# RWKV-7 chunks and dropless experts on one core: a planned order with shared PSUM banks, page balance, later weights, and the first sums on GpSimd

## Chip, core and metric
One NeuronCore of a Trainium2 chip. The metric is the device time of one launch in microseconds; the kernel before takes 901.5 us (median of three runs, 900.42 to 902.14).

## The reference
Two blocks in a row, all float32. The first is a linear-attention recurrence over 768 steps for 4 batches x 8 heads, with a 40 x 40 state per head; the second sends each of the 3072 rows (320 wide) to the best of 8 experts.

```python
for t in range(S):
    y[:, :, t] = einsum('bhd,bhde->bhe', r_t, state)
    Sa = einsum('bhde,bhe->bhd', state, a_t)
    state = state * w_t[:, :, None, :] - einsum('bhd,bhe->bhde', Sa, b_t) + einsum('bhd,bhe->bhde', v_t, k_t)
x = y.transpose(0, 2, 1, 3).reshape(B * S, H * D)
e = argmax(x @ w_gate); p = softmax(x @ w_gate)[e]
out = p * (relu(x @ w1[e]) @ w2[e])
```

## The kernel before
**Units.** The attention part works in 24 units: 12 chunks of 64 steps, for two halves of the batch (`unit(u)`, u = 2·chunk + half). A unit loads seven blocks of 160 KB (decay, K, A, B, V twice, R), four DMAs each. From the decay VectorE makes running products: the scan `rv` (line 432), its reciprocal (437) and the scan `q` (440). GpSimd multiplies K and B (447, two halves) and A (449) by them. TensorE then makes K·A, masked to Gk (464), and B·A in both orientations, masked to T and N (481). The inverse of I + N is built by doubling: the squares of T and N, the first sums I + T (line 505, function `sums`, instructions at 488 and 491), then rounds that each make a power, copy it out, and add to the sum; the last round gives M and TT, and their product is TF. From it come u (641), z (masked to ZU, 663), y and the new state (689). A late step turns y to rows, makes the gate's logits, and SyncE stores 128 rows to memory.

Each fp32 matmul of a 64 x 64 tile stands in the trace as two weight loads and two matmuls, so a step of 16 such products is 32 + 32 instructions. `TILES` makes four neighbouring products use the four quarters of the array; K·A alternates over two of them. All matmul steps are recorded at line 385 (transposes at 573 and 583), all copies out of PSUM at 380 (ScalarE) and 382 (VectorE), all zeros at 350 to 358.

**Order.** Every operation is a `Step` (line 192) with a rank, an engine (ANY is ScalarE or VectorE), a planned cost, and what it reads and writes. `in_order` (212) plays the steps through a small model and emits each engine's instructions in the order in which the model starts them: of all ready steps, the one that can start earliest, then the one of lowest rank. Ranks are the unit's number, u - 3 for loads, u - 1 for the scans and products, u + 1 for the late steps. Hence a step without a predecessor goes as soon as its engine would be idle. The model also hands out PSUM: a step that opens a block of 1 or 2 of the 8 banks waits until such a block is free. For TensorE it counts pages of instructions (`PAGE, FETCH = 256, 3.6`, line 183; `n` is the number of instructions of a step): the next page may be entered 3.6 us after the last one was. On the chip the queues run in this order, each engine waiting on semaphores.

Tiles come from rings (line 320 on): A, R, KB, Vu of three buffers, V2, decay, rv of two, q of three. A load of unit u waits for the readers of the buffer's last use. SyncE issues nearly all loads; ScalarE those of B, A and R of unit 0 (line 424).

**Beginning.** GpSimd first fills constants, among them those that only the routing after the attention part uses (`before`, `ones_sq`, `zero_e`, `keep`, the counted ones at 127 and 128, `tokc`, `tokv`; lines 87 to 147) and `turn_gate` (150 to 157, with two loads from ScalarE's queue). Then come the zeros of the rings as steps of rank -100 to -50, on GpSimd and VectorE. The first expert's weights (2.3 MB) are a SyncE step of rank 8 without a predecessor (`first_weights`, 751).

**After.** Routing (763 to 867) sorts the rows, and the expert part (870 to 987) gathers, multiplies and scatters them.

Of the kernel before, what the change touches and what calls it, by code (L numbers as in the profile page):

```python
# [23 lines left out]
def kernel(  # L24
# [23 lines left out]
    nc = tc.nc  # L48
# [38 lines left out]
    before = consts.tile([128, 128], F32)  # L87
    nc.gpsimd.memset(before[:], 1.0)
    nc.gpsimd.affine_select(
        before[:], before[:], compare_op=ALU.is_gt, fill=0.0, base=0, pattern=[[1, 128]], channel_multiplier=-1,  # L90
    )

# [22 lines left out]

    ones_sq = consts.tile([128, 128], F32)
    nc.gpsimd.memset(ones_sq[:], 1.0)
    zero_e = consts.tile([128, E], F32)
    nc.gpsimd.memset(zero_e[:], 0.0)
    keep = consts.tile([128, E, NT], F32)  # L120
    nc.gpsimd.memset(keep[:], 1.0)
    nc.gpsimd.memset(keep[:, :, 0:1], 0.0)

    def counted(name, shape, pattern, base, mult=0):
        ti = consts.tile(shape, I32, name=name + "_i")
        tf = consts.tile(shape, F32, name=name)
        nc.gpsimd.iota(ti[:], pattern=pattern, base=base, channel_multiplier=mult)
        nc.gpsimd.tensor_copy(tf[:], ti[:])
        return tf
# [9 lines left out]
    iota_r = consts.tile([128, 128], F16)  # L139
    nc.gpsimd.tensor_copy(iota_r[:], iota_f[:])  # L140
# [3 lines left out]
    nc.gpsimd.tensor_scalar(tokc[HP:], tokc[HP:], scalar1=float(S - C), scalar2=None, op0=ALU.add)  # L144
    tokv = consts.tile([128, NT], F32)
    nc.gpsimd.tensor_copy(tokv[:, :NCH], tokc[:])
    nc.gpsimd.tensor_scalar(tokv[:, NCH:], tokc[:], scalar1=-1.0, scalar2=None, op0=ALU.mult)
# [3 lines left out]
    nc.gpsimd.memset(turn_gate[:, :, 128:], 0.0)  # L151
    for par in range(2):
        nc.scalar.dma_start(
            turn_gate[par * HP : par * HP + D, :, 128:], moe_w_gate.rearrange("(p a e) n -> a e p n", a=2, e=D)[par],
        )
    nc.gpsimd.tensor_scalar(turn_gate[:, :, 128:], turn_gate[:, :, 128:], scalar1=-1.0, scalar2=None, op0=ALU.mult)
    nc.gpsimd.tensor_copy(turn_gate[:, :, :128], ident[:, None, :].to_broadcast([128, NP, 128]))
# [25 lines left out]
    PAGE, FETCH = 256, 3.6  # L183
# [28 lines left out]
    def in_order():  # L212
# [3 lines left out]
        page = [0, 0.0]  # L216
# [26 lines left out]
        while ready:  # L243
            times = sorted({f for f in bank_free if f is not None})
            best = None
            for s, r in ready.items():
                new = [h for h in s.ps if h.at is None]
                for e in ((ACT, DVE) if s.eng == ANY else (s.eng,)):
# [13 lines left out]
                    key = (t0, s.rank, t0 + cost)  # L262
# [38 lines left out]
    with tc.tile_pool(name="ring", bufs=1) as ring, \  # L301
# [23 lines left out]
        r_dec = Ring("dec", [SEG * C1 + 1], 2)  # L325
# [34 lines left out]
        for i in range(3):  # L360
            for j, r in enumerate((r_KB, r_A, r_V2, r_Vu, r_R)):
                if i < len(r.bufs):
                    t, held = r.bufs[i]
                    for lo in (32, 96):
                        zero(-99 + 9 * i + j, POOL if lo == 32 else DVE, 0.5, t[lo : lo + 32], held)
        for t, held in r_qini.bufs:
            zero(-98, POOL, 0.6, t[:], held)
        for r in (r_rhs, r_ST, r_S):
            for t, held in r.bufs:
                zero(-50, POOL, 0.6, t[:], held)  # L370
# [4 lines left out]
        def pair(h, width):  # L375
            return psum[:, h.at : h.at + 2, : NP * width].rearrange("x a (p d) -> x a p d", p=NP)
# [18 lines left out]
        def unit(u):  # L395
# [28 lines left out]
            other = ACT if u == 0 else SP  # L424
# [14 lines left out]
            Step(pre, DVE, 0.3, invert, reads=hrv, writes=hqi + hpc)  # L439
# [17 lines left out]

            def p_ka(e, ps=ps):
# [4 lines left out]
            Step(u, PE, 8 * ROUND, p_ka, reads=hKB + hA, writes=[ps], n=64)  # L463
            Step(u, DVE, 0.69, lambda e, ps=ps: nc.vector.tensor_tensor(
                Gk[:], psum[:, ps.at, :].rearrange("x (q p j) -> x q p j", p=NP, q=2),
                m_plus[:, None, None, :].to_broadcast([128, 2, NP, C]), op=ALU.mult,
            ), reads=[ps], writes=hGk)
            T1, hT1 = r_T.take()
            N1, hN1 = r_N.take()
            for t1, ht1, mask, turned_ in ((T1, hT1, m_up, False), (N1, hN1, m_low, True)):  # L470
                ps = Held(2)

                def p_n(e, ps=ps, turned_=turned_):
                    t = pair(ps, C)
                    for p in range(NP):
                        for par, z in TILES:
                            q = par ^ z
                            l, r = b_at(p, q, par), head(Aq, p, q, par)
                            mm(t[halves[z], q, p, :], *((r, l) if turned_ else (l, r)))
                Step(u, PE, 4 * ROUND, p_n, reads=hKB + hA, writes=[ps], n=64)  # L480
                Step(u, DVE, 0.69, lambda e, ps=ps, t1=t1, mask=mask: nc.vector.tensor_tensor(  # L481
                    t1[:], pair(ps, C), mask[:, None, None, :].to_broadcast([128, 2, NP, C]), op=ALU.mult,
                ), reads=[ps], writes=ht1)
# [3 lines left out]
            def sums(e, dst, src, old, o):  # L487
                nc.vector.tensor_tensor(dst[:, 0], src[:, 0], old[:, 0], op=ALU.add)  # L488
                for h in range(2):
                    o_ = halves[1 - h]  # L490
                    nc.vector.tensor_tensor(dst[o_, 1], src[o_ if o else halves[h], 1], old[halves[h], 1], op=ALU.add)  # L491
# [530 lines left out]
```

## Time and profile before
| | us |
|---|---|
| median of three runs | 901.5 |
| profiled execution, its own time | 899.75 |
| its span, first to last instruction | 898.0 |
| attention part, to the last row turned (TensorE) | 574.63 + 2.18 |
| TensorE busy in the span (matmul records) | 776.2 |
| VectorE, ScalarE, GpSimd busy | 460.0, 234.5, 173.7 |
| mean granted clock of TensorE | 0.955 |

The 1.75 us between the profiled execution's time and its span lie around the instructions. Busy time is a share of stages that have different limits: TensorE's 86% is some 90% in the attention part, where many small matmuls overlap, little in the routing (572 to 620 us), and nearly full in the expert part. A granted clock of 1.00 is TensorE's upper level of 2.4 GHz, 0.5 the lower of 1.2 GHz, and a stretch's value is the mean. In rows on stretches the columns are the stretch, its length, then busy time and instructions of TensorE's matmuls, its weight loads, VectorE, ScalarE and GpSimd, the mean clock, the share of the DMA engines and GB/s. "Issue" ahead of an instruction is time in which its engine waited for nothing that the profile shows.

### The profile page before, as it was taken

The page shows a single profiled execution, that of the slowest core. Times are in us where ns is not written, and L with a number is a line of the kernel's source. Part 1 is how long each engine was busy: PE and PEld are TensorE (multiplying, and loading weights), DVE is VectorE, ACT ScalarE, POOL GpSimd, SP SyncE. Part 2 cuts the span into 40 slices and gives each one's busy share as a digit, 9 for nine tenths or more (in the row PEclk, how much of TensorE's full clock was granted, in tenths as well). Part 3 has the DMA queues.
Part 4 walks back from the last instruction along what each step waited for, and adds up shares of the span by engine and source line. Part 5 has one row for each costly group of instructions (what it writes and reads, how often), then busy time and mean ns, then how long its engine had stood idle before and what let it go on. Part 6 is the DMA issues. An engine that isn't in the chain of part 4 may idle for free.

```text
span 898.0 us, 38059 instructions
## 1 busy us (share of the span) xinstructions
PE 776.2 (86%) x17128; PEld 606.5 (68%) x17128; DVE 460.0 (51%) x980; ACT 234.5 (26%) x502; POOL 173.7 (19%) x224
## 2 busy tenths in 40 slices
PE   0797789889998999899989998418999999999995
PEld 0686678788887888788878887416845545545543
DVE  6685578777676867687767676361110110120110
ACT  0343244333333334333433433100110110110110
POOL 9332111121202020202020100043211211001001
PEclk9999899999999989999999999656999999999998
DMA  5323313222322232223222200183313513402000
GB/s 165 89 67 86 86 45 69 65 65 60 71 67 61 57 71 64 56 61 75 62 57 60 48 12 12 22 259 96 95 53 107 187 60 114 132 14 83 10 13 23
DMA packets 136569, 65.16 MB, mean 73 GB/s; under 512 B 116881, under 2 KB 132243, under 8 KB 136404
## 3 DMA queue, kind: packets, MB, share of 16 engines
q1 hardware_dynamic: 130888, 52.76, 23.2%
q0 software_dynamic: 3136, 9.44, 3.4%
q8 instruction: 135, 2.21, 1.0%
q10 hardware_dynamic: 2380, 0.50, 0.3%
q14 instruction: 30, 0.25, 0.1%
HBM read 54.01 MB, written 9.31 MB: 71 GB/s over the span
## 4 chain that ended last, share of the span: by engine, by line
issue 36%; PE 30%; DVE 11%; DMA 9%; POOL 7%; SPq 3%; ACT 2%; POOLq 0%; ACTq 0%; DVEq 0%
PE ps L385 25%; DMA dec<-in_packed_dram 8%; PE ps L583 4%; DVE X L491 3%; POOL out_dram L917 3%; SPq L416 3%; POOL xg L875 2%; PE ps L573 2%; ACT X L380 2%; DVE X L488 1%; DVE q L440 1%; DVE T L481 1%; POOL KB L447 1%; DMA KB<-in_packed_dram 1%; DVE TT L491 0%
## 5 line engine op out<-in xcount | busy, mean ns | idle before, releaser
L385 PE MATMUL ps<-X 64*64 64x64 f32 (+1 forms) x6144 | 163.1, 243 | 22.2 <-DVE X L491 10.9
L385 PEld LDWEIGHTS ps<-X 64*64 64x64 f32 x6144 | 133.8, 135 | 42.2 <-DVE X L491 15.4
L901 DVE TENSOR_SCALAR h_sb<-hp 128x448 f32<-128x448 f32 (+2 forms) x44 | 21.8, 497 | 227.1 <-PE hp L900 225.8
L910 PE MATMUL zp<-w,h_sb 128*128 128x320 f32 (+1 forms) x512 | 123.8, 433 | 0.0
L380 ACT COPY X<-ps 128x512 f32<-128x512 f32 x152 | 88.3, 586 | 125.6 <-PE ps L385 119.9
L894 PE MATMUL hp<-xgT,w 128*128 128x448 f32 (+2 forms) x352 | 115.0, 473 | 3.7 <-DVE h_sb L901 2.3
L910 PEld LDWEIGHTS zp<-w,h_sb 128*128 128x128 f32 (+1 forms) x512 | 80.6, 177 | 37.5 <-issue 2.4
L894 PEld LDWEIGHTS hp<-xgT,w 128*128 128x128 f32 x352 | 60.9, 208 | 53.1 <-issue 48.9
L447 POOL TENSOR_TENSOR KB<-KB,rv 128x512 f32<-128x512 f32 x48 | 59.0, 1249 | 133.9 <-DMA A<-in_packed_dram 48.6
L449 POOL TENSOR_TENSOR A<-A,q 128x512 f32<-128x512 f32 x24 | 29.2, 1215 | 248.9 <-PE ps L385 83.8
L917 POOL DMA_INDIRECT out_dram<-zo,s_idx x28 | 27.6, 987 | 185.1 <-ACT zo L916 183.8
L491 DVE TENSOR_TENSOR X<-ps,X 64x256 f32<-64x256 f32 x144 | 60.8, 422 | 3.1
L902 ACT ACTIVATE h_sb<-hp 128x448 f32<-128x448 f32 (+2 forms) x44 | 19.3, 442 | 159.9 <-PE hp L900 121.6
L488 DVE TENSOR_TENSOR X<-ps,X 128x256 f32<-128x256 f32 x72 | 30.4, 422 | 46.4 <-ACT X L380 45.8
L385 PE MATMUL ps<-R,Vu 64*128 64x64 f32 x768 | 51.0, 284 | 2.5 <-issue 1.2
L385 PE MATMUL ps<-A,KB 64*64 64x64 f32 x1536 | 45.3, 224 | 9.0 <-DVE M L524 8.4
L385 PEld LDWEIGHTS ps<-R,Vu 64*128 64x128 f32 x768 | 47.4, 196 | 5.0 <-issue 2.4
L385 PEld LDWEIGHTS ps<-A,KB 64*64 64x64 f32 x1536 | 40.6, 138 | 12.0 <-DVE M L524 8.6
L432 DVE TENSOR_TENSOR_SCAN rv<-dec,ones 128x521 f32<-128x521 f32 x24 | 29.7, 1239 | 34.7 <-DMA dec<-in_packed_dram 22.8
L663 DVE TENSOR_TENSOR ZU<-ps,m_plus 128x512 f32<-128x512 f32 x48 | 30.9, 685 | 28.8 <-PE ps L385 28.6
L916 ACT COPY zo<-zp 128x320 f32<-128x320 f32 x28 | 11.9, 425 | 119.8 <-PE zp L910 115.9
L385 PE MATMUL ps<-ZU,nKB 128*64 128x104 f32 (+1 forms) x768 | 39.6, 257 | 1.0 <-DVE ZU L663 0.8
(178 smaller groups left out, 1066.1 us busy)
## 6 DMA issues: line engine op xcount, KB each, us to landing
w<-in_moe_w_dram SPq DMA_DIRECT2D x8, 1280.0 KB
w<-in_moe_w_dram SPq DMA_DIRECT2D x8, 1024.0 KB
KB<-in_packed_dram SPq DMA_DIRECT2D x188, 40.0 KB
x_rows<-xs SPq DMA_DIRECT2D x48, 96.0 KB
dec<-in_packed_dram SPq DMA_DIRECT2D x96, 40.0 KB
V<-in_packed_dram SPq DMA_DIRECT2D x96, 40.0 KB
Vu<-in_packed_dram SPq DMA_DIRECT2D x96, 40.0 KB
A<-in_packed_dram SPq DMA_DIRECT2D x92, 40.0 KB
```

The source lines that it names most:

```text
L380: nc.scalar.copy(dst, src)
L385: nc.tensor.matmul(out_, lhsT=lhsT, rhs=rhs, start=start, stop=stop, skip_group_check=True)
L432: Step(pre, DVE, 1.4, lambda e: nc.vector.tensor_tensor_scan(rv[:, : SEG * C1 + 1][:, ::-1], dec[:, ::-1], ones65[:, ::-1], 0.0, op0=ALU.m ...
L447: Step(pre, POOL, 1.25, lambda e, kb=kb, by=by: nc.gpsimd.tensor_tensor(kb, kb, by, op=ALU.mult), reads=hrv, writes=hKB[i : i + 1])
L449: Step(pre, POOL, 1.22, lambda e: nc.gpsimd.tensor_tensor(Aq[:], Aq[:], q3[:, :, :C], op=ALU.mult), reads=hq, writes=hA)
L488: nc.vector.tensor_tensor(dst[:, 0], src[:, 0], old[:, 0], op=ALU.add)
L491: nc.vector.tensor_tensor(dst[o_, 1], src[o_ if o else halves[h], 1], old[halves[h], 1], op=ALU.add)
L583: nc.tensor.transpose(psum[:, ps.at + b // NP, b % NP * 128 : (b % NP + 1) * 128], at(*divmod(b, 2)).rearrange("x s t -> x (s t)"), ident[:],)
L663: Step(u, DVE, 0.69, lambda e, s=s, ps=ps: nc.vector.tensor_tensor(ZU[:, s, :, :C], psum[:, ps.at + s, :].rearrange("x (b j) -> x b j", j= ...
L894: nc.tensor.matmul(hp[:, : c1 - c0], lhsT=w[0][:, db, (fb + i) * 128 : (fb + i + 1) * 128], rhs=xT[:, db, c0:c1], start=(db == 0), stop=False,
L910: nc.tensor.matmul(zp[r0 : r0 + n], lhsT=h[:, fb, c0 : c0 + n], rhs=w[2][:, fb, :], start=(fb == 0), stop=(fb == FB - 1), skip_group_check ...
L917: ins_ = nc.gpsimd.indirect_dma_start(out=out[:, :], out_offset=bass.IndirectOffsetOnAxis(ap=si, axis=0), in_=zo[:], in_offset=None, bound ...
```

## The change
- `in_order`: among steps that can start at the same time, the rank has a term `uneven` added: how far TensorE's cost would run off from `PACE` (0.0134 us) per instruction. The first page counts as holding 190 instructions.
- Costs of steps are set anew: sums 1.29 (from 1.1), transposes 0.59 and 1.02, z 1.93, the row turn 1.12, K·A 1.0, large zeros 0.9.
- The two orientations of B·A become one step of 128 instructions into one block of two banks (T in the first half of each bank, N in the second; the products alternate); the two squares likewise, one after the other; and in the last round the sum, then the power. Masks and copies wait for the whole step.
- The state's share of y (`p_yr`) is no longer a step ahead of z, but the first half of y's step.
- The first sums I + T are a GpSimd step (cost 1.9) instead of a VectorE step.
- The routing constants become one GpSimd step of rank 12 (cost 8); `turn_gate` is filled by steps of rank -80 and -1, its two loads issued by GpSimd. The zeros' ranks change.
- The decay ring has three buffers; ScalarE's queue issues B, A and R of units 0 and 1.
- The first expert's weights wait for the last step of unit 12.

```diff
-    PAGE, FETCH = 256, 3.6
+    PAGE, FETCH, FIRST = 256, 3.6, 190
+    PACE = 0.0134
-        page = [0, 0.0]
+        page = [FIRST, FETCH]
+        even = 0.0
...
-                    key = (t0, s.rank, t0 + cost)
+                    uneven = 2 * abs(even + s.cost - s.n * PACE) if s.n else 0.0
+                    key = (t0, s.rank[0] + uneven, s.rank, t0 + cost)
...
+            if s.n:
+                even = min(1.0, max(-1.0, even + s.cost - s.n * PACE))
...
-    for par in range(2):
-        nc.scalar.dma_start(
+    def fill_turn_gate(e):
+        nc.gpsimd.memset(turn_gate[:, :, 128:], 0.0)
+        for par in range(2):
+            nc.gpsimd.dma_start(
...
-        r_dec = Ring("dec", [SEG * C1 + 1], 2)
+        r_dec = Ring("dec", [SEG * C1 + 1], 3)
...
+        h_tg = Held()
+        Step(-80, POOL, 1.5, fill_turn_gate, writes=[h_tg], lag=3)
+        Step(-1, POOL, 0.2, turn_sign, writes=[h_tg])
+        Step(12, POOL, 8, route_constants)
...
-            other = ACT if u == 0 else SP
+            other = ACT if u < 2 else SP
...
-            for t1, ht1, mask, turned_ in ((T1, hT1, m_up, False), (N1, hN1, m_low, True)):
-                ps = Held(2)
-                Step(u, PE, 4 * ROUND, p_n, reads=hKB + hA, writes=[ps], n=64)
+            ps = Held(2)
+            def p_n(e, ps=ps):
+                for p in range(NP):
+                    for par, z in TILES:
+                        q = par ^ z
+                        l, r = b_at(p, q, par), head(Aq, p, q, par)
+                        mm(pair(ps, C, 0)[halves[z], q, p, :], l, r)
+                        mm(pair(ps, C, 1)[halves[z], q, p, :], r, l)
+            Step(u, PE, 8 * ROUND, p_n, reads=hKB + hA, writes=[ps], n=128)
+            for w, t1, ht1, mask in ((0, T1, hT1, m_up), (1, N1, hN1, m_low)):
+                masked(u, DVE, t1[:], ht1, ps, lambda w=w, ps=ps: pair(ps, C, w), mask[:, None, None, :].to_broadcast([128, 2, NP, C]))
...
             def sums(e, dst, src, old, o):
-                nc.vector.tensor_tensor(dst[:, 0], src[:, 0], old[:, 0], op=ALU.add)
+                eng = nc.gpsimd if e == POOL else nc.vector
+                eng.tensor_tensor(dst[:, 0], src[:, 0], old[:, 0], op=ALU.add)
...
-                Step(u, PE, 4 * ROUND, p_sq, reads=hN1 + hT1, writes=[ps], n=64)
+            Step(u, PE, 8 * ROUND, p_sq, reads=hN1 + hT1, writes=[ps], n=128)
-            Step(u, DVE, 1.1, lambda e, X=X: sums(e, X[:, :, :, 2, :], ihalf[:, None, None, :].to_broadcast([128, 2, NP, C]), T1[:], False),
+            Step(u, POOL, 1.9, lambda e, X=X: sums(e, X[:, :, :, 2, :], ihalf[:, None, None, :].to_broadcast([128, 2, NP, C]), T1[:], False),
...
+            def p_end(e, ps=ps, X=X):
+                p_sum(e, pair(ps, C, 1).unsqueeze(3), X, 1)
+                p_power(e, pair(ps, C, 0), X, 1, 0)
+            Step(u, PE, 8 * ROUND, p_end, reads=hX, writes=[ps], n=128)
...
-                before_z = [Step(u, PE, 4 * ROUND, p_yr, reads=hSn + hR, writes=[psy], n=64)]
...
             def p_y(e):
+                if c:
+                    for p in range(NP):
+                        for q, par in TILES:
+                            mm(y_at()[halves[par], q, p, :C], Sn[halves[q], p, par, :], R_[halves[q], p, par, :], start=(p == 0), stop=False)
...
+            if u == NU // 2:
+                half_way = steps[-1]
...
-        Step(8, SP, 2.0, first_weights)
+        Step(8, SP, 2.0, first_weights, after=[half_way])
```

## Rows read from the trace of the kernel before
**Rows 1.** Stretches: busy us (instructions) of each engine, granted clock, DMA share, GB/s
```profile
80.00:120.00 40.00, 27.60 (x858) 24.39 (x850) 21.60 (x45) 11.42 (x25) 8.00 (x9) 0.87 0.33 75
120.00:560.00 440.00, 402.26 (x13249) 359.50 (x13251) 320.64 (x676) 164.69 (x350) 66.95 (x71) 0.99 0.25 57
...
545.00:561.00 16.00, 14.27 (x547) 12.83 (x548) 8.29 (x16) 5.29 (x10) 0.00 (x0) 1.00 0.02 4
```
**Rows 2.** The page, parts 1 and 3: instructions of each engine; the instruction queue
```profile
PE 776.2 (86%) x17128; PEld 606.5 (68%) x17128; DVE 460.0 (51%) x980; ACT 234.5 (26%) x502; POOL 173.7 (19%) x224
...
q8 instruction: 135, 2.21, 1.0%
```
**Rows 3.** TensorE's waits in 120 to 560 us: us in total, times, longest
```profile
PE ps L385 <- issue: 11.5, 17, 1.2
PE ps L385 <- DVE X L491: 9.1, 20, 0.6
...
PE ps L385 <- DVE TT L491: 1.5, 5, 0.3
```
**Rows 4.** Groups of instructions, shapes apart: busy us, mean ns | idle before
```profile
L491 DVE TENSOR_TENSOR X<-ps,X 64x256 f32<-64x256 f32 x144 | 60.8, 422 | 3.1
...
L917 POOL DMA_INDIRECT out_dram<-zo,s_idx x28 | 27.6, 987 | 185.1 <-ACT zo L916 183.8 <-issue 1.2
...
L491 DVE TENSOR_TENSOR X<-ihalf,T 64x256 f32<-64x256 f32 x48 | 20.2, 421 | 0.7
...
L488 DVE TENSOR_TENSOR X<-ihalf,T 128x256 f32<-128x256 f32 x24 | 12.5, 523 | 0.1
```
**Rows 5.** Timeline of SyncE's queue, the beginning: start, us, what
```profile
0.80 0.44 SPq L170 DMA_DIRECT2D w<-in_moe_w_dram  x1
...
3.28 15.61 SPq L416 DMA_DIRECT2D dec<-in_packed_dram  x8
```
**Rows 6.** Chain that ended last: start, us, what
```profile
3.28 7.70 DMA dec<-in_packed_dram
...
248.92 1.70 DMA dec<-in_packed_dram
```
**Rows 7.** Timeline of GpSimd, the beginning
```profile
1.43 0.28 POOL L89 TENSOR_SCALAR_AFFINE_SELECT before<-before 128x128 f32<-128x128 f32 x1
...
3.84 0.20 POOL L117 MEMSET ones_sq<- 128x128 f32 x1
...
8.96 0.25 POOL L147 TENSOR_SCALAR tokv<-tokc 128x12 f32<-128x12 f32 x1
...
11.77 0.29 POOL L156 TENSOR_SCALAR turn_gate<-turn_gate 128x32 f32<-128x32 f32 x1 [0.92 <-DMA turn_gate<-in_moe_w_gate_dram]
...
23.93 2.52 POOL L447 TENSOR_TENSOR KB<-KB,rv 128x512 f32<-128x512 f32 x2 [1.08 <-DMA KB<-in_packed_dram]
```
**Rows 8.** Timeline of VectorE, 60 to 130 us
```profile
90.30 1.24 DVE L432 TENSOR_TENSOR_SCAN rv<-dec,ones 128x521 f32<-128x521 f32 x1 [8.40 <-DMA dec<-in_packed_dram]
...
102.28 1.24 DVE L432 TENSOR_TENSOR_SCAN rv<-dec,ones 128x521 f32<-128x521 f32 x1 [4.75 <-DMA dec<-in_packed_dram]
```
**Rows 9.** VectorE's waits in 120 to 560 us
```profile
DVE rv L432 <- issue: 9.7, 3, 5.1
...
DVE rv L432 <- DMA dec<-in_packed_dram: 4.1, 5, 2.0
```
**Rows 10.** Timeline of TensorE: halves of T and N, then K·A
```profile
157.45 0.65 PE L385 MATMUL ps<-A,KB 64*64 64x64 f32 x32
157.91 0.65 PE L385 MATMUL ps<-KB,A 64*64 64x64 f32 x32
...
180.65 1.15 PE L385 MATMUL ps<-A,KB 64*64 64x64 f32 x32
```
**Rows 11.** GpSimd's waits in 120 to 560 us
```profile
POOL KB L447 <- DMA A<-in_packed_dram: 48.6, 5, 14.3
...
POOL KB L447 <- DMA KB<-in_packed_dram: 15.5, 5, 7.1
```

More of the change, by code (lines that the diff above doesn't have):

```diff
@@ L151, with route_constants @@
-    nc.gpsimd.memset(turn_gate[:, :, 128:], 0.0)
-    for par in range(2):
-        nc.scalar.dma_start(
[L154 to L157, printed above, removed]
+    def route_constants(e):
+        nc.gpsimd.memset(before[:], 1.0)
+        nc.gpsimd.affine_select(
+            before[:], before[:], compare_op=ALU.is_gt, fill=0.0, base=0, pattern=[[1, 128]], channel_multiplier=-1,
+        )
+        nc.gpsimd.memset(ones_sq[:], 1.0)
+        nc.gpsimd.memset(zero_e[:], 0.0)
+        nc.gpsimd.memset(keep[:], 1.0)
+        nc.gpsimd.memset(keep[:, :, 0:1], 0.0)
+        for ti, tf, pattern, base, mult in iotas:
+            nc.gpsimd.iota(ti[:], pattern=pattern, base=base, channel_multiplier=mult)
+            nc.gpsimd.tensor_copy(tf[:], ti[:])
+        nc.gpsimd.tensor_copy(iota_r[:], iota_f[:])
+        nc.gpsimd.tensor_scalar(tokc[HP:], tokc[HP:], scalar1=float(S - C), scalar2=None, op0=ALU.add)
+        nc.gpsimd.tensor_copy(tokv[:, :NCH], tokc[:])
+        nc.gpsimd.tensor_scalar(tokv[:, NCH:], tokc[:], scalar1=-1.0, scalar2=None, op0=ALU.mult)
@@ L456, in unit, with masked @@
             ps = Held(1)
+            def masked(u, by, t, held, ps, src, mask):
+                if by == DVE:
+                    Step(u, DVE, 0.69, lambda e: nc.vector.tensor_tensor(t, src(), mask, op=ALU.mult), reads=[ps], writes=held)
+                else:
+                    Step(u, ACT, 0.59, lambda e: nc.scalar.copy(t, src()), reads=[ps], writes=held)
+                    Step(u, POOL, 1.2, lambda e: nc.gpsimd.tensor_tensor(t, t, mask, op=ALU.mult), writes=held)
             def p_ka(e, ps=ps):
@@ L468, in unit @@
+            masked(u, DVE, Gk[:], hGk, ps, lambda ps=ps: psum[:, ps.at, :].rearrange("x (q p j) -> x q p j", p=NP, q=2),
+                   m_plus[:, None, None, :].to_broadcast([128, 2, NP, C]))
             T1, hT1 = r_T.take()
             N1, hN1 = r_N.take()
[L470 to L483 removed]
+            ps = Held(2)
@@ L493, in unit, with p_sq @@
             X, hX = r_X.take()
-            for i, (l, r) in enumerate(((T1, N1), (N1, T1))):
-                ps = Held(2)
-                def p_sq(e, ps=ps, l=l, r=r):
-                    t = pair(ps, C)
+            ps = Held(2)
+            def p_sq(e, ps=ps):
+                for w, (l, r) in enumerate(((T1, N1), (N1, T1))):
                     for p in range(NP):
@@ new lines, in unit @@
+                Step(u, DVE, 1.29, lambda e, ps=ps, X=X, Xn=Xn: sums(
+                    e, Xn[:, :, :, 2, :], half_sums(ps, 2)[:, :, :, 1, :], X[:, :, :, 2, :], True,
+                ), reads=[ps] + hX[2:3], writes=hXn[2:3])
+                X, hX = Xn, hXn
+                k *= 2
+            M, hM = r_M.take()
+            TT, hTT = r_TT.take()
+            ps = Held(2)
+            def p_end(e, ps=ps, X=X):
+                p_sum(e, pair(ps, C, 1).unsqueeze(3), X, 1)
+                p_power(e, pair(ps, C, 0), X, 1, 0)
@@ L554, in unit @@
+            Step(u, PE, 8 * ROUND, p_end, reads=hX, writes=[ps], n=128)
+            Step(u, DVE, 1.29, lambda e, ps=ps, X=X, TT=TT: sums(e, TT[:], pair(ps, C, 1), X[:, :, :, 2, :], True), reads=[ps] + hX[2:3], writes=hTT)
+            Step(u, DVE, 0.69, lambda e, ps=ps, M=M: nc.vector.tensor_tensor(M[:], pair(ps, C, 0), eye(2, NP), op=ALU.add), reads=[ps], writes=hM)
             TF, hTF = r_TF.take()
```

129 lines of the change are left out of this document (47 added, 82 removed).

## The prediction
> **What bounds the kernel now.** I read the stretches first, because the attention part (0 to about 572 us) and the expert part after it have nothing in common, and the change touches only the first. In 120 to 560 us VectorE works 320.64 us of 440 and TensorE shows 402.26, so TensorE is the nearest to a bound and VectorE the next [rows 1]. The reader should not take 91% busy for a full TensorE: over those 440 us it issues 13249 matmuls and 13251 weight loads, 26500 instructions, one every 16.6 ns, while in 545 to 561 us it issues 1095 in 16 us, one every 14.6 ns [rows 1]. Its instructions come in pages: the instruction queue moved 135 packets [rows 2] for the 34256 instructions of TensorE (17128 matmuls, as many weight loads), 254 a packet, so 16.6 ns is 4.22 us a page and the best stretch 3.71 us. The planner that writes the order down assumes 256 and 3.6 us (line 183).
>
> Then the waits of TensorE in the same stretch: 11.5 us for nothing the profile shows ("issue"), and behind it 9.1 us and 1.5 us for the last additions on VectorE, L491 [rows 3]. The planner costs that group of three additions at 1.1 us; two of 422 ns and one of about the same are 1.27 us [rows 4], so TensorE is sent ahead too early.
>
> Last, the beginning. SyncE issues the first expert's weights at 0.80 us, ahead of all inputs, and then spends 15.61 us on the first eight decay loads [rows 5]; the first of them takes 7.70 us, against 1.70 us for one at 248.92 us [rows 6]. GpSimd multiplies nothing before 23.93 us [rows 7]. The late queue is felt again later: in 80 to 120 us TensorE is busy 27.60 of 40 us at a mean clock of 0.87 of its upper level [rows 1], and VectorE stands for 8.40 us and 4.75 us in front of a scan whose decay has not landed [rows 8].
>
> **The change, part by part.** All terms are against the profiled execution, 899.75 us, which is 1.75 us under the median of 901.5.
>
> *Start.* The routing constants leave GpSimd's front. Twenty-five of them run from 3.84 us to the one that starts at 8.96 us, and two make a triangle before them [rows 7]; without the other work between them they fill 4.2 us. The wait of 0.92 us ahead of the sign of the gate weights [rows 7] goes too, since that step now follows the other zeros. Against this the two gate loads are issued by GpSimd: its queue's issues of another kind take 987 ns [rows 4], so 2 us. GpSimd's zeros ended near 22.9 us and it then waited 1.08 us for the load of K [rows 7]; that load comes earlier, as nothing stands in front of the decays and three loads of the second unit move to ScalarE's queue, which has no work yet. Zeros end near 22.9 - 5.1 + 2 = 19.8 us, so the first multiply starts 4.2 us sooner: **-4.2 us**. The bounds are 0 (another load is late) and -10 (the planner lets the multiply pass some zeros). ScalarE's issues are hidden by its idle front; if it had work there, they would hold it for as long as SyncE's take.
>
> *Constants later.* As one step of rank 12 without a predecessor they are taken as soon as GpSimd would be idle, so early, and whatever is queued behind them on GpSimd (a multiplication of K and B, or the new sums) waits up to 4.2 us once. **+1 us**, bounds 0 and +4.2.
>
> *Queue and third decay buffer.* With no weights first, three loads fewer and the decay loaded a unit earlier, the two stalls of VectorE in 80 to 105 us should go. In 120 to 560 us TensorE is idle 37.74 of 440 us [rows 1], which would be 3.4 us of 40; here it is 12.4 us. So 9 us are to be had, and some more for the clock; **-9 us**, bounds 0 (a different load is late next, K and B behind the same SyncE queue) and -12. After 120 us VectorE waits another 9.7 + 4.1 us in front of that scan [rows 9]; a fifth of it reaching TensorE is **-3 us**, bounds 0 and -13.8.
>
> *Order by pages and truer costs.* The L491 waits, 10.6 us, I take as mostly gone by the cost 1.29 in place of 1.1 and by putting the sum first in the last round: **-9 us**. Of the 11.5 us of issue half: **-6 us**. The lower bound for both is 0. The upper is the whole distance to the best rate: 26500 x (16.6 - 14.6) ns = 53 us.
>
> *Shared banks.* T and N, the two squares, and the last power and sum now each take one pair of banks in place of two, and the state's share of y no longer opens its pair before z. That leaves the order more freedom, which I don't price. It has two costs. T's mask can't start until N's matmuls are done: the second half starts 0.46 us after the first [rows 10], three times in a unit, about 1.4 us of added latency, hidden by the neighbouring unit's work, but 33 us over 24 units were that cover gone; 0 taken. And T's and N's matmuls now alternate on the same quarter of the array. Nothing shows that pattern; the nearest rows are the same 32 matmuls over four quarters in turn (0.65 us) and over two (1.15 us) [rows 10]. Bounds: 0, and 2 x 0.5 us x 24 = 24 us. At 14.6 ns an instruction, 128 instructions need 1.87 us to arrive anyway, which covers most of 2 x 1.15; **+3 us**.
>
> *First sums on GpSimd.* VectorE loses 20.2 + 12.5 us [rows 4], 7% of its time. On GpSimd the multiplication of twice the size takes 1.26 us (two in 2.52) [rows 7], so an addition some 0.63 us, estimated by size, three of them 1.9 us, 45 us in all. GpSimd works 66.95 us of 440 [rows 1], so it has room. The sums are due when both squares are copied out: N's mask, 128 matmuls and a copy, 2.5 us or more after T. I take **0**; the cover is that GpSimd is free at that moment. Without it: the rival below. The other bound is a gain of 10 us where VectorE was last.
>
> *Weights later.* After unit 12, four issues on SyncE, and the decay load behind them takes 7.70 us in place of 1.70 [rows 6]: 6 us, mostly covered by the third buffer. **+2 us**, bounds 0 and +6; the weights are needed only in the expert part, 250 us later. Nothing in the expert part changes.
>
> Sum: -4.2 + 1 - 9 - 3 - 9 - 6 + 3 + 0 + 2 = **-25 us**: 874.6 us, as a median 876.
>
> **Rivals.**
>
> *Supply at its best.* If freed banks and balanced pages bring the whole stretch near the best stretch, two thirds of 53 us come in place of the 18 us of the three steady terms: 876 - 35 + 18, about 859; with all terms at their better ends 845. For: 14.6 ns is reached in stretches. Against: the order has to hold it for 24 units.
>
> *Pages were never the limit.* Most pages take longer than the best ones, and issue is only 11.5 us. Then balance gives nothing and the added delays count: without the 6 us 882, with half of the 33 us of latency above 890 to 899. The Trainium skill, "Runtime: NRT & Kernel Launch", section "Instruction fetch mechanics", speaks for this: the sequencer fetches the next 256 instructions while it runs the current ones, and crossing into them is said to be mostly hidden. By that rule the balance is worth 0 and the result 882. The gap between 16.6 and 14.6 ns agrees that supply isn't always what limits; that the rate never gets better than 14.6 ns for long speaks against the rule.
>
> *GpSimd becomes the wait (slower).* In 120 to 560 us GpSimd stands 48.6 us in five waits in front of the K/B multiplication for the loads of A, and 15.5 us in five for K/B itself, up to 14.3 us each [rows 11]. These waits cost nothing now, since the products are early. But the sums of the current unit stand in the same queue: behind such a wait they hold the inverse's first round and what is queued behind it on TensorE, since both queues run in order. Were all 64 us passed on, 876 + 64 = 940; it decides from 25 us on, two fifths of it; at 35 us the result is 911.
>
> *The order is only different.* Waits move from one place to another, the start alone is better: 897 to 901.
>
> **How the numbers follow.** Forecast (858 to 892): 0.55. Supply at its best: 0.15. Pages no limit with added latency (882 to 899): 0.13. GpSimd: 0.11. Only different: 0.06. About 0.2%, 1.8 us, is what a measurement of this kernel tells from no change. Faster is the first three and a little of the last, 0.83; same 0.05; slower 0.12. The range leaves out the far ends of GpSimd's and of the best supply's: 848 to 904.
>
> **What would show it.** Right: the first multiplication of K and B near 19.8 us instead of 23.93; no wait of VectorE over 2 us in front of the decay scan; 80 to 120 us at the upper clock throughout; TensorE's waits for L491 below 4 us; under 16 ns an instruction between 120 us and the end of the attention part, which ends 25 us sooner; the expert part as long as before. Wrong: waits of TensorE for GpSimd's sums above a few us; T's and N's 64 matmuls taking over 2 us; a dip after unit 12; or the same 16.6 ns with other names in front of the waits.

## The result, and the profile after

The changed kernel takes 872.96 us (median of 4 runs, 870.45 to 878.37); the kernel before, run beside it, 901.82 us (4 runs, 900.42 to 903.75). The ratio is 0.9687 with an interval of [0.9636, 0.9737]. The forecast was 876.0, between 848 and 904, with 0.83 for faster. A run over 1.5% longer than the fastest of its kernel is left out of every ratio, and the times given for the experiments below are medians of the runs that count. The profiled execution took 873.95 us, its span 872.2, against 899.75 and 898.0 before: 25.8 us to be found.

Stretches of the kernel before that were not shown yet; columns as in [rows 1].

```profile
0.00:40.00 40.00, 13.85 (x437) 12.07 (x438) 24.10 (x47) 6.39 (x10) 28.16 (x74) 1.00 0.50 131
40.00:80.00 40.00, 37.16 (x1240) 33.11 (x1239) 34.70 (x72) 17.51 (x38) 10.61 (x9) 1.00 0.37 84
...
120.00:520.00 400.00, 365.80 (x11960) 326.70 (x11960) 294.32 (x620) 149.11 (x319) 66.47 (x69) 0.99 0.27 61
```

The same view of the kernel after.

```profile
0.00:40.00 40.00, 15.21 (x320) 14.00 (x322) 26.14 (x48) 4.56 (x7) 33.62 (x80) 0.91 0.40 87
40.00:80.00 40.00, 30.91 (x1049) 28.16 (x1052) 26.49 (x49) 14.23 (x28) 14.36 (x15) 0.91 0.31 71
80.00:120.00 40.00, 38.84 (x1336) 35.34 (x1328) 31.37 (x68) 16.23 (x37) 12.12 (x15) 1.00 0.28 65
120.00:520.00 400.00, 376.31 (x12561) 343.02 (x12550) 287.67 (x606) 146.78 (x319) 106.81 (x128) 0.97 0.30 69
```

The first transposition of the expert part, before and then after (timelines of TensorE).

```profile
603.77 0.87 PE L883 MATMUL tp<-ident,xg 128*128 128x128 f32 x3 [5.14 <-DMA xg<-x_rows,g_idx]
...
579.35 0.88 PE L903 MATMUL tp<-ident,xg 128*128 128x128 f32 x3 [5.05 <-DMA xg<-x_rows,g_idx]
```

Both kernels issue the same 17128 matmuls, so counting them at fixed times is the cleanest way to see who is ahead. At 40 us the changed kernel is behind, 320 against 437. The hole of 80 to 120 us in [rows 1] (858) is gone (1336), but 40 to 80 us has lost 191. At 120 us it is 320 + 1049 + 1336 = 2705 against 437 + 1240 + 858 = 2535: 170 matmuls ahead, at 400 us / 12561 = 31.8 ns each 5.4 us. From 120 to 520 us it gains 601 more, 19.1 us; an instruction takes 400 us / 25111 = 15.9 ns, against 16.7 before in this stretch. Together 24.5 us of the 25.8. The expert part starts 24.4 us sooner and takes nearly what it took: 872.2 - 579.35 = 292.9 us against 898.0 - 603.77 = 294.2.

The 19.1 us have two parts. TensorE's idle time in 120 to 520 us falls from 400 - 365.80 = 34.2 to 23.7 us, and a matmul takes 376.31 us / 12561 = 30.0 ns of busy time in place of 365.80 us / 11960 = 30.6, which over 12561 matmuls is some 8 us. What makes the second is not shown.

The beginning after the change: GpSimd's first multiplication, SyncE's first loads, VectorE, TensorE (timelines of four engines).

```profile
20.98 3.32 POOL L468 TENSOR_TENSOR KB<-KB,rv 128x512 f32<-128x512 f32 x2
...
2.59 9.40 SPq L437 DMA_DIRECT2D dec<-in_packed_dram  x8
12.08 1.66 SPq L437 DMA_DIRECT2D V<-in_packed_dram  x4
...
30.71 1.25 DVE L453 TENSOR_TENSOR_SCAN rv<-dec,ones 128x521 f32<-128x521 f32 x1 [4.18 <-DMA dec<-in_packed_dram]
31.87 0.67 DVE L482 TENSOR_TENSOR T<-ps,m_up 128x512 f32<-128x512 f32 x1
32.45 0.68 DVE L482 TENSOR_TENSOR Gk<-ps,m_plus 128x512 f32<-128x512 f32 x1
...
33.19 1.09 PE L406 MATMUL ps<-nV,Gk 64*64 64x40 f32 x32 [2.86 <-DVE Gk L482]
```

SyncE is through the first eight decay DMAs (two loads) 6.2 us faster than in [rows 5], and the first multiplication starts at 20.98 us instead of 23.93 [rows 7]. But then VectorE reaches the scan of a later unit and stands 4.18 us for its decay; the masks T and Gk of the current unit are behind it in the queue, and TensorE waits 2.86 us for Gk. That is where the head start goes. Note also what the SyncE rows say side by side: four DMAs of V take 1.66 us of the queue, eight of a decay 9.40.

Later the same picture: VectorE's scans (timeline), then the stretches up to and after two falls of the clock.

```profile
70.37 1.78 DVE L453 TENSOR_TENSOR_SCAN rv<-dec,ones 128x521 f32<-128x521 f32 x1 [5.77 <-DMA dec<-in_packed_dram]
...
166.07 1.24 DVE L453 TENSOR_TENSOR_SCAN rv<-dec,ones 128x521 f32<-128x521 f32 x1 [3.55 <-DMA dec<-in_packed_dram]
...
66.00:73.40 7.40, 2.67 (x137) 2.20 (x134) 3.03 (x4) 1.75 (x4) 4.43 (x5) 1.00 0.29 67
73.40:76.80 3.40, 3.40 (x44) 3.15 (x48) 2.01 (x5) 0.42 (x1) 0.00 (x0) 0.51 0.46 105
162.00:168.90 6.90, 4.92 (x187) 4.66 (x182) 3.29 (x7) 1.11 (x3) 0.00 (x0) 1.00 0.29 65
168.90:175.80 6.90, 6.21 (x144) 5.69 (x136) 4.03 (x8) 1.07 (x2) 2.17 (x3) 0.51 0.26 61
```

While VectorE stands in front of the scan, TensorE is busy 2.67 us of 7.40; behind that its clock is at the lower level for 3.4 us. In the second case it is there for 6.9 us, with 144 matmuls where 31.8 ns each would give 217, so some 2.3 us are lost on top. In these two cases the wait for one decay is paid twice. It isn't always: behind the next long wait TensorE, which stayed busy during it, kept the upper level (1.00 from 231.40 to 238.20 us).

```profile
231.41 1.24 DVE L453 TENSOR_TENSOR_SCAN rv<-dec,ones 128x521 f32<-128x521 f32 x1 [5.14 <-DMA dec<-in_packed_dram]
```

Waits between 120 and 560 us, TensorE's and then VectorE's in front of the scan.

```profile
PE ps L406 <- issue: 10.0, 14, 1.4
...
PE ps L406 <- DVE X L517: 1.3, 3, 0.5
...
DVE rv L453 <- DMA dec<-in_packed_dram: 25.0, 11, 5.1
DVE rv L453 <- issue: 3.2, 1, 3.2
```

Against [rows 3] the waits for the last additions (L491 before, L517 now) fell from 10.6 to 1.3 us, while those for issue hardly moved, from 11.5 to 10.0. These are waits for pages: each of the 14 ends 1.2 to 1.7 us after a packet of the instruction queue has landed (so do the 17 of the kernel before), and in the changed kernel no two of these packets start less than 3.3 us apart. Against [rows 9] the scan's waits rose from 13.8 to 28.2 us: the third decay buffer did not end them.

Two small readings. The 64 matmuls that alternate between T and N (timeline of TensorE; the last row is the next step), and the first sums on GpSimd (groups, and GpSimd's wait in front of them, 120 to 560 us):

```profile
336.45 0.36 PE L406 MATMUL ps<-A,KB 64*64 64x64 f32 x8
336.62 0.32 PE L406 MATMUL ps<-KB,A 64*64 64x64 f32 x8
...
337.55 0.98 PE L406 MATMUL ps<-A,KB 64*64 64x64 f32 x28
...
L517 POOL TENSOR_TENSOR X<-ihalf,T 64x256 f32<-64x256 f32 x48 | 36.0, 750 | 3.3
...
L514 POOL TENSOR_TENSOR X<-ihalf,T 128x256 f32<-128x256 f32 x24 | 17.6, 734 | 121.0 <-DVE T L482 121.0
...
POOL X L514 <- DVE T L482: 107.7, 17, 12.7
```

Alternating costs 337.55 - 336.45 = 1.10 us against 2 x 0.46 [rows 10], some 0.2 us. GpSimd waits 107.7 us for T, and no wait for GpSimd's sums stands among TensorE's: GpSimd is early.

### The profile page after: what moved, and what is told of

Same layout as the page of the kernel before. It is cut to its first block, busy times and chain, and to the rows that moved or that the text cites. A ratio compares the mean times of both kernels' runs of the same rounds, so it can differ in the third digit from the quotient of the medians.

```text
span 872.2 us, 38097 instructions
## 1 busy us (share of the span) xinstructions
PE 770.5 (88%) x17128; PEld 611.2 (70%) x17128; DVE 440.1 (50%) x931; ACT 222.3 (25%) x483; POOL 227.1 (26%) x298
## 4 chain that ended last, share of the span: by engine, by line
PE 38%; issue 34%; DVE 8%; DMA 8%; POOL 7%; SPq 2%; ACT 1%; POOLq 0%; DVEq 0%; ACTq 0%
PE ps L406 33%; DMA dec<-in_packed_dram 7%; PE ps L604 4%; POOL out_dram L937 3%; POOL xg L895 3%; PE ps L594 1%; SPq L437 1%; DVE X L517 1%; ACT X L401 1%; DVE rv L453 1%; DVE q L461 1%; DVE Gk L482 1%; DVE TT L517 0%; DMA V<-in_packed_dram 0%; DVE M L574 0%
## 5 line engine op out<-in xcount | busy, mean ns | idle before, releaser
L406 PE MATMUL ps<-X 64*64 64x64 f32 (+1 forms) x6144 | 160.0, 246 | 8.8 <-DVE X L403 3.7
L406 PEld LDWEIGHTS ps<-X 64*64 64x64 f32 x6144 | 136.4, 137 | 20.8 <-issue 8.6
L401 ACT COPY X<-ps 128x512 f32<-128x512 f32 x163 | 93.2, 587 | 164.4 <-PE ps L406 150.6
L930 PEld LDWEIGHTS zp<-w,h_sb 128*128 128x128 f32 (+1 forms) x512 | 80.6, 177 | 37.4 <-issue 2.4
L468 POOL TENSOR_TENSOR KB<-KB,rv 128x512 f32<-128x512 f32 x48 | 57.0, 1206 | 63.7 <-DMA KB<-in_packed_dram 34.2
L517 DVE TENSOR_TENSOR X<-ps,X 64x256 f32<-64x256 f32 x144 | 60.8, 422 | 3.2
L406 PE MATMUL ps<-A,KB 64*64 64x64 f32 x1536 | 58.3, 233 | 1.2 <-issue 1.2
L406 PE MATMUL ps<-R,Vu 64*128 64x64 f32 x768 | 53.5, 291 | 5.4 <-DVE Gk L482 2.5
L406 PEld LDWEIGHTS ps<-A,KB 64*64 64x64 f32 x1536 | 54.2, 142 | 3.8 <-issue 3.3
L406 PEld LDWEIGHTS ps<-R,Vu 64*128 64x128 f32 x768 | 49.7, 203 | 8.3 <-DVE Gk L482 2.6
L453 DVE TENSOR_TENSOR_SCAN rv<-dec,ones 128x521 f32<-128x521 f32 x24 | 31.5, 1311 | 42.9 <-DMA dec<-in_packed_dram 37.4
L514 POOL TENSOR_TENSOR X<-ihalf,T 128x256 f32<-128x256 f32 x24 | 17.6, 734 | 121.0 <-DVE T L482 121.0
L406 PE MATMUL ps<-ZU,nKB 128*64 128x104 f32 (+1 forms) x768 | 42.4, 266 | 5.8 <-DVE ZU L677 4.6
L406 PEld LDWEIGHTS ps<-ZU,nKB 128*64 128x64 f32 x768 | 37.0, 146 | 8.1 <-issue 6.2
```

Of the source, the lines that this page charges most:

```text
L401: nc.scalar.copy(dst, src)
L406: nc.tensor.matmul(out_, lhsT=lhsT, rhs=rhs, start=start, stop=stop, skip_group_check=True)
L453: Step(pre, DVE, 1.4, lambda e: nc.vector.tensor_tensor_scan(rv[:, : SEG * C1 + 1][:, ::-1], dec[:, ::-1], ones65[:, ::-1], 0.0, op0=ALU.m ...
L468: Step(pre, POOL, 1.25, lambda e, kb=kb, by=by: nc.gpsimd.tensor_tensor(kb, kb, by, op=ALU.mult), reads=hrv, writes=hKB[i : i + 1])
L514: eng.tensor_tensor(dst[:, 0], src[:, 0], old[:, 0], op=ALU.add)
L517: eng.tensor_tensor(dst[o_, 1], src[o_ if o else halves[h], 1], old[halves[h], 1], op=ALU.add)
```

## The experiments

All ratios are to the kernel before, timed beside each run; that kernel itself ran between 893 and 908 us there, so the 0.2% of the prediction was too fine. An edit of the planner's costs, ranks or buffers reshuffles the whole planned order, which sets how finely such a run can be read. The weights' edit and the order of the decay's DMAs, below, don't.

**The small parts, one undone at a time.**

```diff
-            Step(u, POOL, 1.9, lambda e, X=X: sums(...
+            Step(u, DVE, 1.29, lambda e, X=X: sums(...
```


> The changed kernel with the first sums back on VectorE (cost 1.29), all else kept. Theory (the sums on GpSimd are worth about nothing, since VectorE has idle time and GpSimd is free when they are due): within 5 us of the changed kernel's 873, TensorE's waits for L517 still under 4 us. Rival A (VectorE's 33 us were on the path): 8 to 20 us slower than the changed kernel, with longer waits for VectorE. Rival B (GpSimd's queue holds the sums up): 5 to 15 us faster.

868.43 us, ratio 0.9622 [0.9532, 0.9712]: the sums on GpSimd are worth nothing that can be told.

```diff
-        Step(8, SP, 2.0, first_weights, after=[half_way])
+        Step(8, SP, 2.0, first_weights)
```


> The changed kernel with the first expert's weights issued first again. Theory (they cost the start about 6 us, and half-way they cost some 3 to 6 us in the clock dip of 340 to 360 us): 0 to 8 us slower, the first decay load over 6 us again, no bulk transfer and no dip near 340 us. Rival (the later weights are what made the kernel faster): 12 us slower or more. Rival 2 (half-way costs as much as the start): the same within 2 us.

876.79 us, 0.9706 [0.9613, 0.9799]. This edit leaves the order on every engine but SyncE as it was. Up to 40 us TensorE does far less (first row, 120 matmuls where the changed kernel did 320), yet 200 matmuls, 6.4 us, show in the end as 2 to 4 us, which the intervals don't tell from nothing. The other side of it is the second row, of the changed kernel: right behind its four issues of the weights the DMA engines are full, the clock is at the lower level and TensorE does 98 matmuls in 6.8 us; with the weights first it does 195 there, at a clock of 1.00.

```profile
0.00:40.00 40.00, 8.31 (x120) 7.33 (x120) 21.29 (x41) 3.62 (x5) 26.11 (x51) 0.99 0.53 135
...
343.00:349.80 6.80, 6.80 (x98) 6.32 (x95) 3.75 (x8) 1.62 (x3) 2.16 (x3) 0.50 1.01 289
```

```diff
-        r_dec = Ring("dec", [SEG * C1 + 1], 3)
+        r_dec = Ring("dec", [SEG * C1 + 1], 2)
```


> The changed kernel with two decay buffers. In the changed kernel the scan still waits for the decay in most units, 42 us between 30 and 530 us. Theory (the lateness comes from the four serial loads being planned as 1.7 us when they take 4.4, not from the buffer): within 5 us of the changed kernel, VectorE's waits in front of the scan 35 to 60 us. Rival (the third buffer holds the gain): 8 us slower or more, waits over 70 us.

869.5 us, 0.9664 [0.9586, 0.9743]: the third buffer is worth nothing that can be told, and the scan's waits between 30 and 530 us are not longer without it (27 us against 42). The three medians lie between 868 and 877 us; a difference of 8 us between two orders is therefore not read as an effect of an edit.

**Balance, costs, banks.**

```diff
-                    uneven = 2 * abs(even + s.cost - s.n * PACE) if s.n else 0.0
+                    uneven = 0.0
```


> The changed kernel with the balance term of the order set to 0; costs, shared banks and all else kept. Theory (half of the issue waits, about 6 us, come from it): 3 to 10 us slower, instructions between 120 and 530 us one every 16.1 to 16.3 ns. Rival A (pages are hidden, the balance is worth nothing): within 2 us. Rival B (it is most of the gain): 15 us slower or more.

890.21 us, 0.989 [0.9791, 0.9989]: 17 us of the 29 are gone, twice the spread above, which is rival B's time. TensorE's work in the long stretch and its first waits (120 to 560 us) in this run:

```profile
120.00:520.00 400.00, 363.20 (x12152) 331.54 (x12148) 282.65 (x584) 146.40 (x313) 106.05 (x124) 0.97 0.30 69
...
PE ps L406 <- issue: 14.2, 21, 1.5
PE ps L406 <- DVE M L574: 6.7, 4, 3.8
```

16.5 ns an instruction on average, nearly the rate of before. In the changed kernel, undoing the balance costs more than any other single part. But of these 17 us less than a third is pages. A matmul takes the same busy time as with it (363.20 us / 12152 = 29.9 ns, against 30.0); TensorE is idle for 36.8 us in place of 23.7. Of these 13.1 us the waits for issue give some 5 (14.2 and, ahead of transpositions, 1.1 us to 560 us, against 10.0); the rest are waits for other engines, such as 6.7 us for M, 0.5 with the balance. The next run puts it alone on the kernel before (the lines of the diff with `FIRST`, `PACE`, `even`, `uneven`, nothing else):

> The kernel before with the page-balanced choice alone (and the page count that starts at 190): no shared banks, the old costs, constants first, two decay buffers, sums on VectorE, weights early. Theory 'balance is most of the gain, on any order': 880 to 888 us, the ratio to the kernel before about 0.98, and under 16.1 ns a matmul between 120 and 520 us (16.6 before). Rival 'balance needs the truer costs and the larger groups to know what it balances': 895 to 905 us and 16.5 ns a matmul.

936.42 us, 1.0377 [1.033, 1.0423]: neither theory; it makes that kernel slower. The loss is in the plan already. By the planner's own model (`in_order` played through, the costs being equal within each pair) TensorE's attention part ends at 507 us in the kernel before and at 535 with the balance, and at 494 in the changed kernel and at 522 without it. Are the old costs to blame? The truer costs alone on the kernel before, and both together:

```diff
-                Step(u, DVE, 1.1, lambda e, ps=ps, X=X, w=w, dst=dst: sums(
+                Step(u, DVE, 1.29, lambda e, ps=ps, X=X, w=w, dst=dst: sums(
...
-            Step(u, PE, 1.71, p_z, reads=hV + huT + hR, writes=[ps], after=before_z, n=64)
+            Step(u, PE, 1.93, p_z, reads=hV + huT + hR, writes=[ps], after=before_z, n=64)
-            Step(u, PE, 8 * 2 * w / 2400, p_y, reads=hnKB + (hZU[:2] if last else hZU), writes=[psy], n=64)
+            Step(u, PE, 16 * 0.95 * w / 1000, p_y, reads=hnKB + (hZU[:2] if last else hZU), writes=[psy], n=64)
...
```


> The kernel before with the truer costs alone (invert 0.4, sums 1.29, pairs 0.59, turned 1.02, Z 1.93, y 0.5 and 1.58, gate 1.12, scaling 0.39, the filling of KB and Vu 0.9). Theory 'a planner that knows the costs places the steps well by itself': 885 to 893 us, and TensorE's waits for X built by L491 (10.2 us) under 5. Rival 'the costs are only there for the balance to work on': 898 to 905 us, waits as before.

> The kernel before with the truer costs and the page-balanced choice together, nothing else. Theory 'balance works only on true costs, and the two carry the gain': 872 to 882 us, where balance on the old costs gave 936; under 16.1 ns a matmul between 120 and 520 us. Rival 'balance also needs the larger groups of the shared banks, or the freer queues': over 890 us.

Costs alone 912.74 us, 1.0091 [1.0052, 1.013]; with balance 935.13 us, 1.0371 [1.0325, 1.0417]. Both theories fall. With the costs alone TensorE's waits for X of L491 do get shorter, 6.4 us in place of 10.2, without a gain; the second run's rival (over 890 us) has its time. The waits of TensorE and of VectorE (120 to 560 us) with costs and balance on the kernel before (there the sums are L493 and L496, copies L385, the scan L437):

```profile
PE ps L390 <- ACT X L385: 12.1, 21, 0.8
PE ps L390 <- DVE M L529: 7.2, 9, 3.8
...
PE ps L390 <- issue: 4.6, 5, 2.0
...
DVE rv L437 <- DMA dec<-in_packed_dram: 39.3, 16, 5.4
```

The balance does its own work here, issue waits fall from 11.5 [rows 3] to 4.6 us; what it pays with is a list of waits for the unit's own chain, and later decays. Next, the banks: T and N, the squares, and M and TT apart again, all else as changed.

```diff
-            Step(u, PE, 8 * ROUND, p_n, reads=hKB + hA, writes=[ps], n=128)
             for w, t1, ht1, mask in ((0, T1, hT1, m_up), (1, N1, hN1, m_low)):
...
+                ps = Held(2)
...
+                Step(u, PE, 4 * ROUND, p_n, reads=hKB + hA, writes=[ps], n=64)
```


> The changed kernel with T and N, their squares, and M and TT each in a group of banks of its own again, in groups of 64 matmuls; balance, costs and all else as in the changed kernel. Theory 'shared banks pay little by themselves': 870 to 880 us, within 0.8% of the changed kernel. Rival 'the larger groups are what lets the order be balanced and the waits for X fall': 884 us or more, with TensorE's waits for X in 30 to 530 us back from 1.7 us towards 10.

867.08 us, 0.9633 [0.9567, 0.97]: the sharing of T and N, the squares, and M and TT is worth nothing that can be told; TensorE's waits for the last sums stay at 1.9 us (30 to 530 us). So balance pays in the changed kernel (-17 us) and costs 33 in the one before, and neither the costs nor these banks make the difference; undone singly, nor do the sums, the weights or the third buffer. What is left in the diff is y's step (with z no longer behind its first half), the sum ahead of the power in the last round, and the front. The first of them is plain in the trace: from the first part of y (`R,S`) to its second (`ZU,nKB`), one unit in the kernel before, one after.

```profile
198.80 0.64 PE L385 MATMUL ps<-R,S 64*64 64x64 f32 x32
217.68 1.65 PE L385 MATMUL ps<-ZU,nKB 128*64 128x104 f32 x32
```
```profile
216.75 0.65 PE L406 MATMUL ps<-R,S 64*64 64x64 f32 x32
217.32 1.65 PE L406 MATMUL ps<-ZU,nKB 128*64 128x104 f32 x32
```

In this unit a pair of banks, one of four, is open from 198.80 to 217.68 + 1.65 = 219.33 us, 20.5 us for 2.3 us of matmuls; after, it is 2.2 us. In the run with costs and balance on the kernel before, the planned order puts each unit's first part ahead of the second part of the unit before it, so that the first part at 223.72 us has its second at 257.59:

```profile
223.72 0.64 PE L390 MATMUL ps<-R,S 64*64 64x64 f32 x32
...
257.59 3.04 PE L390 MATMUL ps<-ZU,nKB 128*64 128x104 f32 x32
```

36.9 us here. Over the 22 units with a first part the median is 19.9 us in the kernel before, 17.6 with the costs alone, 31.5 with balance alone, 33.8 with both, and 2.5 in the changed kernel. With a unit every 24 us or so, the two slowest kernels hold more than one of the four pairs for y on average, and a step that the planner holds back for a bank can show in the trace as a later link of its unit's chain, not as a wait of its own. So y's step is the likeliest thing that the balance needs from the rest of the change. It is not shown: y's step, the order in the last round and the front were not tried one by one.

**The decay load.** The remaining scan waits pointed at SyncE. Its timeline and its waits in the changed kernel:

```profile
24.81 4.40 SPq L437 DMA_DIRECT2D dec<-in_packed_dram  x4
...
SPq L437 <- DMA dec<-in_packed_dram: 76.6, 49, 3.1
```

Four DMAs of a decay hold the queue for 4.40 us, four of equal size of V, shown above, 1.66; 49 waits in 24 loads say why: twice in a load, a decay DMA waits for another decay DMA. The planner counts 1.7 us for every load. A cure was tried in two ways. First the order of the four DMAs, so that two that wait for one another are not neighbours:

```diff
-                    for par in range(2):
-                        for q in range(2):
+                    for par, q in ([(0, 0), (1, 0), (0, 1), (1, 1)] if n == 0 else [(0, 0), (0, 1), (1, 0), (1, 1)]):
```


> Only the order of a decay load's four DMAs changes: the two that wait for one another in a pair are no longer issued back to back. Theory 'the scan waits come from the slow, serial decay load': a decay load takes SyncE about 2.8 us and not 4.2, the 37.4 us in 15 waits of VectorE for dec (30 to 530 us) fall below 25 us, TensorE's clock falls less often than seven times, and the kernel takes 3 to 8 us less than the 873 us of the changed kernel (about 867). Rival 'the waits are where the planned order puts the load, not how long it takes': the waits and the time stay within 3 us of the changed kernel's.

Then only the planned cost:

```diff
-                Step(u - 3, eng, 1.7, fn, writes=held, lag=2.5)
+                Step(u - 3, eng, 4.2 if n == 0 else 1.7, fn, writes=held, lag=2.5)
```


> The planner is told that a decay load takes 4.2 us of its queue instead of 1.7; nothing else changes. Theory 'the planned order puts decay loads too late because it costs them too low': the waits of VectorE for dec fall below 20 us in 30 to 530 us and the kernel takes about 865 us. Rival 'the decay load is paced by its buffer and by SyncE's own waits for others': the waits stay above 30 us and the time is 870 us or more.

847.87 us, 0.9394 [0.9347, 0.9442], and 853.1 us, 0.9449 [0.9405, 0.9493]. Both give more than the theory asked: 25 and 20 us beyond the changed kernel. The first is the cleanest run of all, since the planner doesn't see the order inside a load: the engines' work and SyncE's loads come in the order of the changed kernel. In the profiled executions 16.1 and 16.3 us lie ahead of the expert part, which starts at 563.29 and 563.04 us; the rest lies in the expert part, which neither edit touches. SyncE's load, the stretches, the waits from 120 to 520 us and the start of the expert part with the new order; last, SyncE's waits with the new cost:

```profile
2.59 5.78 SPq L436 DMA_DIRECT2D dec<-in_packed_dram  x8
...
SPq L436 <- DMA dec<-in_packed_dram: 35.1, 31, 2.9
...
0.00:40.00 40.00, 14.87 (x508) 13.47 (x508) 30.69 (x54) 7.15 (x12) 35.53 (x81) 1.00 0.41 91
40.00:80.00 40.00, 33.95 (x1180) 30.72 (x1176) 28.76 (x60) 16.30 (x33) 16.79 (x16) 1.00 0.38 86
80.00:120.00 40.00, 38.70 (x1341) 35.18 (x1338) 31.28 (x66) 16.02 (x35) 12.61 (x14) 1.00 0.29 66
120.00:520.00 400.00, 376.37 (x12780) 340.78 (x12780) 292.15 (x614) 149.15 (x324) 105.33 (x126) 1.00 0.29 68
...
DVE rv L452 <- DMA dec<-in_packed_dram: 6.0, 3, 3.9
...
PE ps L406 <- issue: 20.6, 27, 2.0
...
563.29 0.87 PE L902 MATMUL tp<-ident,xg 128*128 128x128 f32 x3 [5.07 <-DMA xg<-x_rows,g_idx]
...
SPq L437 <- DMA dec<-in_packed_dram: 77.5, 48, 3.1
```

Eight decay DMAs take 5.78 us of SyncE, not 9.40, and its waits for them fell from 76.6 to 35.1 us; the scan's waits fall from 25.0 to 6.0 us; the clock stays at its upper level in all four stretches; and what TensorE now waits for is issue. By 120 us it has done 3029 matmuls, 324 (10 us) more than the changed kernel. With only the cost changed the loads are as slow (77.5 us of such waits), but the planner issues them sooner, and the scan's waits for the decay fall from 37.4 to 4.5 us (30 to 530 us): what hurt was the 2.5 us by which each load put its queue behind the plan. That is likely also why the third buffer did nothing: a load is late in its queue however many buffers it may choose from.

The new order of the DMAs on the kernel before:

> The kernel before with its decay loads issued in the other order (as in the run that gave 848 us), nothing else. Theory 'the slow decay load holds both kernels': 880 to 890 us, VectorE's waits in front of the decay scan (30.4 us in 30 to 530) down by half or more. Rival 'it only binds where the balanced order lets matmuls run faster than the loads': 897 to 905 us.

887.7 us, 0.9834 [0.978, 0.9888]: 15 us by itself, again with the order as it was, and VectorE's waits in front of the scan fall from 30.4 to 10.2 us (30 to 530 us). So the decay load held the kernel before as well. Last, all that helped or did no harm (new order of the DMAs, planned at 2.6 us, first sums on VectorE):

> The changed kernel with the decay loads in the other order and planned at 2.6 us, and the first sums back on VectorE. Theory 'the scan waits are gone with the order of the loads, and the place of the sums is indifferent': 844 to 852 us. Rival 'VectorE comes under pressure once the decay waits are gone': 855 us or more, with TensorE's waits for X built by the sums over 5 us.

849.55 us, 0.9409 [0.9359, 0.9459]: no better than the new order of the DMAs alone, which beats both kernels by one line and is the version to keep.

## Why the prediction was right, and which steps were not

The time came within 3 us of the forecast, on a sum of terms of which several were wrong against one another: up to 120 us the gain was 5.4 us where the sum had 12.2, behind it more than the sum had. That the total came so near is in part luck.

- *Start, -4.2.* The first multiplication came 2.95 us sooner, not 4.2; the rest was given back at once (117 matmuls behind at 40 us), since the scan's decay was late at 30.71 us. I had counted what the queue gains and not who is next in it.
- *Queue and third buffer, -9, and the scan after 120 us, -3.* The step that failed outright. The hole of 80 to 120 us is gone, but a smaller one stands in 40 to 80; start, constants and queue together gave 5.4 us where the sum had 12.2. After 120 us the waits doubled. A buffer was taken as the cure for a load that is slow in its own queue; [rows 5] already showed it, 15.61 us for eight DMAs, and I read it as the weights' doing. The weights had 6.2 us of it; 9.40 us were left.
- *Truer costs and sum first, -9.* The waits named went as forecast (10.6 to 1.3 us), and TensorE's idle time from 120 to 520 us fell by 10.5 us with those for issue left as they were; this term is the part of the sum that the trace bears out. But the costs alone did not make the kernel before faster (1.0091): a wait that goes is not a gain unless the order has something to put in its place.
- *Balance, -6.* On issue the term was near: the rest of the change brings those waits to 15.3 us and the balance takes some 5 back, so that against the kernel before they fall only from 11.5 to 10.0. But undoing it costs 17 us. The other 12 or so are waits for other engines, which the sum had under no term: the balance earns its place here more by the order that it makes than by the pages it was made for. It also isn't a term of its own: on the kernel before it costs 33 us, with issue waits of 4.1 us.
- *Shared banks, +3, freedom unpriced.* The alternating matmuls cost 0.2 us a unit in the row shown, some 4 us if nothing hid it. The freedom that I left at nothing is worth nothing that can be told for the three shared pairs (the run with banks apart); whether y's step, which I named in half a sentence, has more is open, and likely by the times for which its banks were held.
- *First sums, 0, and weights, +2.* Neither can be told from nothing in the two runs' times. The dip after unit 12, one of the signs of being wrong, is in the trace all the same: 97 matmuls fewer in 6.8 us, some 3 us. GpSimd's additions took 734 and 750 ns, 2.2 us for three and not 1.9.

Of the rivals, "Pages were never the limit" is not what happened: its time, 882 us or more, did not come, and the balance takes some 5 us of waits for pages off the changed kernel. The Trainium skill, "Runtime: NRT & Kernel Launch", section "Instruction fetch mechanics", holds that crossing into the next 256 instructions is mostly hidden. The trace agrees for most pages: from 120 to 520 us the changed kernel fetches 98, and 14 are followed by a wait for issue, 10.0 us in all. It is not so for all: without the balance there are 21 such waits in 96 pages, and with the decay load mended issue is TensorE's first wait, 20.6 us. The 17 us of the run without balance do not decide on the rule, since most of them are other waits. "GpSimd becomes the wait" did not happen: the wait of 107.7 us for T is GpSimd's own and nobody's loss. "Supply at its best" did not happen either. The run with the new order of the decay's DMAs has its time, 848 us, but at 400 us / 25560 = 15.6 ns an instruction. The 14.6 ns, taken for the best rate, were not the best: from 535 to 551 us the kernel before issues 1200 instructions, one every 13.3 ns. "Only different" falls with the ratio.

## What to carry to other kernels

Look at how long a DMA-issuing queue holds each load, and compare equal loads: one that takes 4.4 us where its neighbours take 1.7 is either mended by the order of its DMAs or told to the planner, and either was worth more here than another buffer. A refinement of a planner has no worth of its own (17 us gained on one structure, 33 lost on another), so test it on the one it will run on; here the planner's own end time, 28 us later in either case, told the sign before any run. And count instructions done at fixed times: it shows gains that are given back.

## What was not expected of the hardware

The same DMAs hold their queue for 9.40 us in one order and for 5.78 us in another, with no byte changed, because of waits of one for another. TensorE's clock fell to its lower level for 3.4 or 6.9 us behind two long waits of VectorE around which TensorE had gaps (busy 2.67 of 7.40 and 4.92 of 6.90 us), and stayed at the upper one behind a third, of 5.14 us, during which it had none. The kernel of 848 us, with 11 us of such waits between 30 and 530 us where the changed kernel has 37, kept the upper level from 0 to 520 us. And in the kernels before and after, without balance, and with the new order of the decay's DMAs, each wait of TensorE for nothing that the profile shows ended 1.2 to 1.7 us after a packet of the instruction queue had landed.
